# A Mamba-2 scan and a SwiGLU feed-forward in one kernel: banks of PSUM in pairs, 1024-wide operations, smaller weight pieces, and the first scan's preparation spread over the first gates

## Chip, cores, metric

One core of one Trainium2 chip. The metric is the device time of one execution in microseconds (us). All runs that are compared are of the state "fast"; the cores of the chip other than this one are idle.

## The reference

```python
# per batch and head, chunk by chunk (S = 768, N = 16, D = 32, 4 batches, 8 heads)
L = exp(cum_i - cum_j) * causal           # decay between two positions
M = (C @ B.T) * L                         # "products"
y = M @ x + (C @ state) * exp(cum)        # "outputs"
state = decay * state + sum_j (B_j x_j) * decay_from_j   # "states"

# bridge to 3072 tokens x 256, then
xn = x / sqrt(mean(x*x) + 1e-6) * rms_g
g = xn @ w_gate; val = xn @ w_val         # 256 -> 1536, float64 weights given as words
out = (silu(g) * val) @ w_out             # 1536 -> 256
```

## The kernel before

The tokens go through in six blocks of 512. A block has a gate loop of 12 steps (`gate_val`: two gate and two value matmuls, Silu on ACT, the hidden product `h` on DVE) and an output loop (`project`). The scan of the next block runs between the steps of the gate loop (`scan_steps`), for two pairs of tiles (a tile is 128 positions of one batch). Its exponentials of decays are prepared earlier: for the first blocks by mask-and-sum groups, matmuls that put the causal mask and the sums of logarithms into PSUM. DVE, ACT and POOL are the vector, scalar and GpSimd engines. The weights arrive as 64-bit numbers and are converted to 32 bits by DVE and ACT in pieces (`begin`, `finish`) during the head and block 0.

```python
def bank(name, shape=(128, 512)):                 # five single banks of PSUM
    return mm.tile(list(shape), FP32, tag="shared", bufs=5, name=name)
def pair_of_banks(name):                          # and one pair
    return mm.tile([P, 2, 512], FP32, tag="y", name=name)
# ... cut ...
pieces = [(n, c, w) for c, w in ((0, 128), (128, 128), (256, 256), (512, 512), (1024, 512))
          for n in "gv"]
pieces += [("o", c, 4) for c in range(0, NF, 4)]
# ... cut ...
def decays(g):                                    # exp of the decays of tile g
    L = pair_tile(g)
    for h in range(NH):
        nc.scalar.activation(out=L[:, h], in_=L[:, h], func=AF.Exp, bias=neg[:, c, k:k + 1])
    nc.gpsimd.affine_select(out=L, in_=L, ...)    # causal mask
def products(p, qs, gs=None):                     # qs: which 32-row groups of TensorE
    g = {q: bank("g%d" % q, (P, 2, 2 * P)) for q in qs}
    for i in range(2):
        for q in qs:
            nc.tensor.matmul(out=g[q][:, i], lhsT=s["T"][r, i, 0], rhs=...,
                             tile_position=(32 * q, 0), ...)
    for q in qs:
        nc.vector.tensor_tensor(out=L, in0=g[q], in1=L, op=ALU.mult)
# ... cut: in the loops, a pair's products are one call on all four row groups ...
[(products, p, range(4))],
[(states, p), (scale, q)],
[(turn, q, 0, cp)],
# ... cut: after block 0's output loop ...
for k in range(NT):
    put(blk, k, os[k])
for k in range(NT):
    decays(4 * (blk + 2) + k)
```

## Time and profile before

| | before |
|---|---|
| time | 495.72 us (median of 3), span 494.3 |
| TensorE busy | 465.0 us (94%) |
| first gate matmul | 41.9 us |
| block 0: gate loop, output loop | 64.4, 22.05 us |
| gate loops of blocks 1; 2, 3, 4; 5 | 61.9; 50.2, 50.1, 50.4; 41.2 us |

The gate loop of block 5 has no scan beside it and is 12 steps of 3.43 us with nothing between. Blocks 2 to 4 are the same plus a scan of some 9 us of TensorE. Blocks 0 and 1 show what stands beside that: block 0 is 14 us longer than block 2 and block 1 is 12. With the head of 42 us these are all that a change could win without taking work off TensorE. The lines are in the prediction.

### The profile page before, as it was taken

To read this page: it belongs to the slowest core of one execution; us is meant where nothing else is said; L and a number is where in the kernel's file an instruction comes from. 1 tells how busy PE (TensorE), PEld (TensorE's weight loads), DVE (VectorE), ACT (ScalarE), POOL (GpSimd) and SP (SyncE) were. 2 spreads that over 40 slices of the span, in tenths; PEclk is the share of its full clock that TensorE was granted. 3 is DMA by queue.
4 is the path that set the end of the run, shared out by engine and by line. 5 is a ranking of instruction groups with operands and counts; after the bars stand their busy time and mean duration, and the time that the engine had idled before them with its cause. 6 is when DMAs were issued, how large, how long until landed. Compare 5 with 4: busy or idle time off the path is not lost.

```text
span 494.3 us, 6025 instructions
## 1 busy us (share of the span) xinstructions
PE 465.0 (94%) x2410; PEld 274.8 (56%) x2410; DVE 156.2 (32%) x284; ACT 159.1 (32%) x325; POOL 42.1 (9%) x72
## 2 busy tenths in 40 slices
PE   6877869999939999999999999999999999999997
PEld 4543324468514447854447844448844448744486
DVE  3465998781014231114140124140124220121100
ACT  2327633530561213651314451223541220111100
POOL 3011000000030000220000310001110000000000
PEclk9989879999969999999999999999999999999999
DMA  9940455920470200063300071200000000000000
GB/s 138 184 113 2 170 170 181 176 78 1 72 141 1 86 0 12 23 83 98 86 1 11 23 112 69 86 2 11 30 3 0 1 1 21 21 1 0 0 12 32
DMA packets 85515, 27.85 MB, mean 56 GB/s; under 512 B 76048, under 2 KB 80336, under 8 KB 85488
## 3 DMA queue, kind: packets, MB, share of 16 engines
q1 hardware_dynamic: 81328, 27.21, 23.6%
q10 hardware_dynamic: 4160, 0.26, 0.6%
q8 instruction: 19, 0.31, 0.2%
q14 instruction: 8, 0.07, 0.0%
HBM read 24.22 MB, written 3.24 MB: 56 GB/s over the span
## 4 chain that ended last, share of the span: by engine, by line
PE 79%; issue 8%; DVE 3%; ACT 2%; POOL 2%; POOLq 0%; ACTq 0%; DVEq 0%
PE gate L478 25%; PE val L478 23%; PE o L489 21%; PE y L419 2%; PE g L357 2%; PE tp L343 2%; PE y L410 1%; POOL L L320 1%; DVE e L163 1%; PE ms L447 1%; PE rb L460 1%; PE A_ps L375 1%; DVE h L486 1%; DVE L L364 0%; POOL rs L452 0%
## 5 line engine op out<-in xcount | busy, mean ns | idle before, releaser
L478 PE MATMUL gate<-xn,wg 128*128 128x512 f32 x288 | 143.6, 622 | 6.2 <-DVE h L486 4.3
L478 PE MATMUL val<-xn,wv 128*128 128x512 f32 x288 | 137.6, 601 | 0.0
L489 PE MATMUL o<-wo,h 128*128 128x256 f32 x576 | 127.4, 380 | 0.0
L489 PEld LDWEIGHTS o<-wo,h 128*128 128x128 f32 x576 | 108.7, 190 | 16.9 <-issue 2.9
L486 DVE TENSOR_TENSOR h<-u,val 128x512 f32<-128x512 f32 x72 | 49.4, 686 | 208.7 <-PE val L478 141.8
L478 PEld LDWEIGHTS val<-xn,wv 128*128 128x128 f32 x288 | 56.1, 195 | 71.9 <-issue 68.5
L481 ACT ACTIVATE u<-gate 128x512 f32<-128x512 f32 x72 | 42.8, 596 | 134.0 <-PE gate L478 98.4
L478 PEld LDWEIGHTS gate<-xn,wg 128*128 128x128 f32 x288 | 52.0, 195 | 56.5 <-issue 44.1
L494 ACT COPY ob<-o 128x256 f32<-128x256 f32 x24 | 8.9, 372 | 107.3 <-PE o L489 89.5
L318 ACT ACTIVATE L<-L,neg 128x128 f32<-128x128 f32 x128 | 38.8, 389 | 0.0
L364 DVE TENSOR_TENSOR L<-g,L 128x512 f32<-128x512 f32 x48 | 30.0, 683 | 8.3 <-PE g L357 8.3
L436 POOL TENSOR_TENSOR sq<-sq 128x256 f32<-128x256 f32 x12 | 9.2, 770 | 254.6 <-ACT sq L435 254.6
L466 DVE SCALAR_TENSOR_TENSOR xn<-yt,gcol,rb 128x512 f32<-128x512 f32 (+1 forms) x14 | 8.8, 669 | 53.6 <-PE rb L460 50.2
L320 POOL TENSOR_SCALAR_AFFINE_SELECT L<-L 128x1024 f32<-128x1024 f32 x16 | 17.5, 1092 | 90.6 <-ACT L L318 90.6
L345 ACT COPY T<-tp 128x512 f32<-128x512 f32 x22 | 12.8, 583 | 33.0 <-PE tp L343 33.0
L435 ACT ACTIVATE sq<-y 128x512 f32<-128x512 f32 x12 | 7.2, 597 | 34.4 <-PE y L410 34.4
L357 PE MATMUL g<-T 32*128 32x256 f32 x192 | 17.8, 404 | 0.4 <-DVE h L486 0.2
L343 PE MATMUL tp<-ident,cp 128*128 128x128 f32 x48 | 9.5, 280 | 7.0 <-POOL cp L329 7.0
L357 PEld LDWEIGHTS g<-T 32*128 32x128 f32 x192 | 10.3, 184 | 10.3 <-issue 7.2
L151 ACT ACTIVATE e<-e,etop 128x1024 f32<-128x1024 int32 (+2 forms) x13 | 11.5, 885 | 10.0 <-DVE e L148 10.0
L419 PE MATMUL y<-L,xr 128*32 128x128 f32 x384 | 13.8, 288 | 0.0
L343 PEld LDWEIGHTS tp<-ident,cp 128*128 128x128 f32 x48 | 6.1, 143 | 13.1 <-POOL cp L329 7.6
(88 smaller groups left out, 234.9 us busy)
## 6 DMA issues: line engine op xcount, KB each, us to landing
L<-rowd SPq DMA_DIRECT2D x16, 512.0 KB, 5.2
xr<-in_x_dram SPq DMA_DIRECT2D x24, 128.0 KB, 3.3
wr<-in_moe_w_out_dram SPq DMA_DIRECT2D x3, 1024.0 KB, 5.4
out_dram<-ob SPq DMA_DIRECT2D x24, 128.0 KB, 1.7
wr<-in_moe_w_gate_dram SPq DMA_DIRECT2D x2, 1024.0 KB, 5.3
wr<-in_moe_w_val_dram SPq DMA_DIRECT2D x2, 1024.0 KB, 4.9
br<-in_B_dram SPq DMA_DIRECT2D x22, 64.0 KB, 3.0
cr<-in_C_dram SPq DMA_DIRECT2D x22, 64.0 KB, 2.9
```

What stands on the lines that cost most here:

```text
L151: nc.scalar.activation(out=ef, in_=e, func=AF.Relu, scale=-8.0, bias=etop)
L318: nc.scalar.activation(out=L[:, h], in_=L[:, h], func=AF.Exp, bias=neg[:, c, k:k + 1])
L320: nc.gpsimd.affine_select(out=L, in_=L, pattern=[[0, NH], [1, P]], compare_op=ALU.is_ge, fill=0.0, base=0, channel_multiplier=-1)
L343: nc.tensor.transpose(out=tp[:, k], in_=src.rearrange("p h n -> p (h n)"), identity=ident)
L345: copy(out=s["T"][:, i], in_=tp)
L357: nc.tensor.matmul(out=g[q][:, i], lhsT=s["T"][r, i, 0], rhs=s["T"][r, i, 1:3].rearrange("p t m -> p (t m)"), start=(i == 0), stop=True, t ...
L364: nc.vector.tensor_tensor(out=L, in0=g[q], in1=L, op=ALU.mult)
L419: nc.tensor.matmul(out=y[o:o + 32, h // 4, i * P:(i + 1) * P], lhsT=s["x"][:, i, h], rhs=Ls[p][:, i, h], start=opens, stop=True, tile_posi ...
L478: nc.tensor.matmul(out=dst, lhsT=w[:, t, fs], rhs=xns[blk][:, t], start=(t == 0), stop=(t == 1))
L481: nc.scalar.activation(out=u, in_=g, func=AF.Silu)
L486: nc.vector.tensor_tensor(out=h, in0=u, in1=v, op=ALU.mult)
L489: nc.tensor.matmul(out=o, lhsT=hs_[blk, f][:, k * P:(k + 1) * P], rhs=wo[:, f], start=(f == 0), stop=(f == NF - 1))
```

## The change

Its intent: keep TensorE fed in the head and in the first two blocks. PSUM is cut anew into two single banks and three pairs; gate and value share a pair, as do the two halves of other results, so that DVE and ACT work on 1024 elements at a time. The weights are converted in smaller pieces with deeper buffers. Block 1's mask-and-sum groups are spread between the first gates (before, they all stood ahead of them; its scan was beside block 0's gate loop already), and the exponentials of block 2 move into block 0's output loop. TensorE gets six dummy matmuls at the start. The core of the diff:

```diff
-        return mm.tile(list(shape), FP32, tag="shared", bufs=5, name=name)
+        return mm.tile(list(shape), FP32, tag="one", bufs=2, name=name)
-        return mm.tile([P, 2, 512], FP32, tag="y", name=name)
+        return mm.tile([P, 2, 512], FP32, tag="pair", bufs=3, name=name)
...
+    pieces = [(n, c, w) for c, w in [(0, 128), (128, 128)] + [(c, 256) for c in range(256, DF, 256)]
+    pieces += [("o", c, 2) for c in range(0, NF, 2)]
...
+    for k in range(6):
+        nc.tensor.matmul(out=idle[:, 0], lhsT=warm[:, 0:P], rhs=warm, start=True, stop=True)
...
-        for h in range(NH):
-            nc.scalar.activation(out=L[:, h], in_=L[:, h], func=AF.Exp, bias=neg[:, c, k:k + 1])
+        nc.vector.tensor_tensor(out=L, in0=L, in1=tok[...].to_broadcast([P, NH, P]), op=ALU.subtract)
+        nc.scalar.activation(out=L, in_=L, func=AF.Exp)
...
-            [(products, p, range(4))],
-            [(states, p), (scale, q)],
-            [(turn, q, 0, cp)],
-            [(outputs, p)],
-            [(turn, q, 1, cp)],
-            [(products, q, range(4))],
+            [(products, p, 0)],
+            [(products, p, 1), (pad, q, pl), (scale, q)],
+            [(states, p), (turn, q, 0, cp)],
+            [(outputs, p), (turn, q, 1, cp)],
+            [(products, q, 0)],
+            [(products, q, 1)],
...
+        if f in (5, 7, 9, 11):           # in block 0's output loop
+            decays(8 + (f - 5) // 2)
```

## The prediction

> **What bounds the kernel now.** I read, in this order: the page's busy rows, the busy time by stretch, the timeline around the two places where TensorE has holes, and the timeline of one undisturbed block. The span is 494.3 us; the timed median is 495.72, so 1.4 us lie outside the span.
>
> ```profile
> PE   6877869999939999999999999999999999999997
> PEclk9989879999969999999999999999999999999999
> ```
>
> Each digit is a fortieth of the span (12.4 us). TensorE is at 9 from the sixth slice on, but for one hole (the 3 in the twelfth slice, 136 to 148 us). So the kernel has two regimes: a head of some 75 us that is bound by latencies and conversions, and a rest that is bound by TensorE.
>
> ```profile
> 54.00:75.00 21.00, 16.50 (x44) 7.21 (x43) 19.92 (x26) 10.62 (x13) 0.00 (x0) 0.76 0.53 190
> 75.00:106.00 31.00, 31.00 (x194) 14.52 (x193) 26.01 (x36) 14.97 (x20) 2.00 (x2) 1.00 0.71 173
> 127.00:143.00 16.00, 8.95 (x27) 4.53 (x25) 0.00 (x0) 14.10 (x40) 5.12 (x8) 0.89 0.75 123
> 212.00:284.70 72.70, 72.70 (x376) 43.48 (x375) 17.59 (x33) 25.17 (x58) 7.75 (x11) 1.00 0.24 51
> ```
>
> (Columns: stretch, length, busy of PE, weight loads, DVE, ACT, POOL with counts, granted clock, DMA.) From 54 to 75 DVE is busy 19.9 of 21 us with converting the weights, and TensorE waits for it, partly at a lower clock (0.76). From 127 to 143 ACT is busy and TensorE is not. Block 2 (212 to 284.7) is TensorE without a hole.
>
> ```profile
> 69.36 3.78 PE L478 MATMUL gate<-xn,wg 128*128 128x512 f32 x4 [4.34 <-DVE h L486]
> ...
> 131.64 9.45 ACT L318 ACTIVATE L<-L,neg 128x128 f32<-128x128 f32 x32
> 141.11 1.28 ACT L481 ACT_TABLE_LOAD   x1
> 142.54 0.71 PE L343 MATMUL tp<-ident,cp 128*128 128x128 f32 x2 [7.05 <-POOL cp L329]
> 144.11 0.48 PE L343 MATMUL tp<-ident,Cd 128*128 128x128 f32 x1 [0.86 <-DVE Cd L332]
> 144.38 3.62 PE L478 MATMUL gate<-xn,wg 128*128 128x512 f32 x4
> ```
>
> The last four rows are the hole at the start of block 1: 32 small exponentials in ACT after block 0, a table load, then TensorE goes on at half speed (3.62 us for a gate that takes 1.9).
>
> From the chain and the timeline, TensorE's schedule is: first gate matmul 41.9; block 0's gates end 106.3; its output matmuls end 128.35; block 1 takes 84.1 (to 212.45); blocks 2, 3, 4 take 72.2, 72.1, 72.5; block 5, which has no scan beside it, 61.9 (to 491.2); copy and store 3.1. Sum 494.3.
>
> **What the Trainium skill says.** "TensorE: Matmul & The Clock Gate", Part 3, says that matmuls on different 32-row groups run at the same time, starting about 4 ns apart. The trace agrees: matmuls of `g` on four row groups start 7 ns apart, and the next four 216 ns later. This decides what splitting them costs. Its Part 1 says that the clock falls to half after an idle window of about 3.4 us; here the records show half speed for 3.4, 3.4, 6.8 and 10.2 us after the holes. "ScalarE: Activation LUTs", What ACT_TABLE_LOAD costs, gives about 1283 ns; every load here takes 1.28 us. "VectorE: DVE Perf Modes", The TRN2 errata, says that each operation pays a fixed cost, so wide ones are cheaper: a 512-wide exponential on ACT takes 608 ns here, the 128-wide one 295 at its pitch (9.45 / 32), so eight of those (2.36 us) become one of about 1.03 (estimate: 608 plus 512 elements at the slope (1149 - 722) / 512 = 0.83 ns of the ACT conversions).
>
> **Part 1: products of the scan, split in two.** Before, `products` of a pair takes all four row groups in one call; after, two calls with two row groups each, on either side of a gate. The trace before holds both forms, the small one in the head:
>
> ```profile
> 226.99 1.15 PE L357 MATMUL g<-T 32*128 32x256 f32 x16
> 228.07 1.98 PE L478 MATMUL gate<-xn,wg 128*128 128x512 f32 x4
> ...
> 22.30 1.13 PE L357 MATMUL g<-T 32*128 32x256 f32 x8
> 23.36 0.43 PE L375 MATMUL A_ps<-xr,Bd 128*32 128x64 f32 x16
> ```
>
> Sixteen instructions on four groups take 1.08 us to the next start, eight on two groups take 1.06. Half the groups means no saving: each call costs the same. The gate after it starts slower too: 1.91 in the chain in place of 1.72, 0.19. So one more call per pair is 1.08 + 0.19 = 1.27 us of TensorE, 2.54 per block, in each of the five blocks that have a scan beside them. DVE's 1024-wide multiplication (about 1.2 us for what took 2 x 0.62) is beside other work and gives nothing back. In blocks 1 to 4 TensorE is the bound, so this is a loss of 4 x 2.54 = 10.2 us; block 0's share is counted below.
>
> **Part 2: the hole of block 1.** The exponentials of block 2 move from after block 0's outputs into its output loop, at its steps 5, 7, 9 and 11, with subtraction on DVE (1.2 each) and one exponential each (1.03); the Silu table is loaded behind them. DVE and ACT idle in that loop now (DVE 4.6 of 21 us busy), so they fit. POOL's padding, for which TensorE waited 7.05 us, then comes some 10 us before it is wanted. The block should fall to the 72.2 of block 2: gain 84.1 - 72.2 = 11.9, less the 2.54 of part 1.
>
> **Part 3: conversions in block 0.** DVE's work per element is the same: 4.87 us for a 1024-wide piece (0.60 + 0.72 + 1.15 + 1.26 + 1.14, starts in the timeline), 2.73 for a 512-wide one. Of the output weights four of six pieces move into the output loop (4 x 2.73 = 10.9 us). DVE's gate loop from the third step on holds 8 gate/value pieces (21.8), parts of two output pieces (4.1), ten hidden products (6), scan (about 7): 39 us, while TensorE has 10 x 3.43 + 9 + 2.5 = about 46. So DVE should no longer bind, save at single pieces.
>
> **Part 4: the head.** TensorE is warmed with 6 dummy matmuls (about 2.6 us at half speed, while it waits 3.2 for `a` anyway). The mask-and-sum groups `e` for four tiles take 2.93 us (34.17 to 37.10). For two tiles I get 2 x 0.216 masks, 8 steps of 0.112, 2 wide passes of 0.43 and about 0.3 of changes: 2.5, again half the groups for nearly the same time. There are four such calls before (11.7 us); after, one of four tiles and six of two (17.9). But only the first and three small ones stand before the outputs of pair 1. Walking the head in TensorE's order with these durations I get: first sums done 9.3 (11.3 before), outputs of pair 1 done 27.3 (34.2 before). Then the norm, now once: square and POOL to 28.8, sums to 29.4, POOL power (1.02) to 30.7, one small `e` group to 31.9, transposes, DVE's two multiplications to 34.0. First gate 34.0 (41.9 before).
>
> Then comes what eats that gain. Before gate 2 can start it needs the pair of banks of gate 0, which waits for `h`, Silu, the Silu table, and ahead of these in ACT the last of block 1's four exponentials. TensorE: gate 0 to 37.4, two `e` groups to 42.4, gate 1 to 45.8, last `e` group to 48.3. Then exponential 1.03, table 1.28, Silu 0.6, `h` 0.68 and handovers: gate 2 at 52.1, against 53.9 before. TensorE idles over 3 us, so I add one cold window (3.4 us at half speed, 1.7 lost). From there 46 us of TensorE work end block 0's gates at 99.6 (106.3 before): gain 6.7. The output loop is 22.05 as before, plus about 0.5 where DVE just misses an output piece at steps 8 and 10.
>
> **Sum.** 99.6 + 22.55 + (72.2 + 2.54) + (216.8 + 7.6) + 61.9 + 3.1 = 486.3 span; with 1.4 outside it 487.7. I say 487.5: 1.7% faster. The gain of 18.6 in the first two blocks (6.7 + 11.9) is more than half paid away by splitting the products in blocks 1 to 4.
>
> **Rivals.**
> - *Splitting costs nothing* (the calls overlap with the gate, or TensorE takes both with its queue): the profile speaks against it (1.06 against 1.08, and a full gate needs all row groups). It would give about 477.
> - *Silu and table do not hold gate 2, no cold window*: for it, the warm start and fewer holes; against it, ACT's strict order. It would save up to 5 us: 482 to 484.
> - *Three pairs are too few*: a gate waits for the third allocation before it (`h`, the multiplication, the copy of `y`). In the full loop each is read about 1 to 2 us after its matmuls and wanted 3 or more later, so I expect no waits; a wait of 0.3 per gate would add 15 us: 502.
> - *The output loop of block 0 starves*: the spread transfers now come after the loads of block 2 on one queue, and DVE, in order, would hold the output weights behind a subtraction that waits for them. They take 5.2 us to land, 8.7 us are there. If late: 2 to 5 us, 490 to 493.
>
> **Range and chances.** The later blocks are counted from rows and good to a microsecond or two; the head is walked by hand and good to some 3. The range is 482.5 to 491.5. The line of 2% is at 485.8, half a deviation below my figure: faster 0.33, same 0.65, slower 0.02.
>
> **What would show it.** Right: `g` as calls of eight instructions with 1.06 to 1.1 us to the next start, blocks 2 to 4 at 74.7 without holes; block 1 also 74.7, with no wait for POOL; a first gate near 34, a hole of some 3 us before gate 2, with a clock below 1 after it; gates of block 0 ending near 99.6. Wrong: blocks 2 to 4 still at 72.2 (part 1 falls, and about 10 us more are won), waits of gates for `h` in every block (three pairs are too few), or block 0's gates ending after 103 (DVE still binds).

## The result

489.61 us (median of 4, 489.46 to 490.0) against 495.94 of the kernel before on the same chip; ratio 0.987 (0.9854 to 0.9888). All ratios here are the mean time of one kernel's fast runs over that of the other's fast runs of the same rounds, so not quite the ratio of the medians. The time lies in the range that was stated, 2 us above the figure, and on the predicted side of the line of 2%.

The slices of the changed kernel's page, for the two rows of the prediction's first fence:

```profile
PE   8989989999999999999999999999999999999997
PEclk9978999999999999999999999999999999999999
```

The hole in the twelfth slice is gone. The clock dips to 7 in the third slice, where the kernel before had 8. By stretch (length, then busy time of PE, weight loads, DVE, ACT, POOL, granted clock, DMA share, GB/s):

```profile
57.00:75.00 18.00, 16.56 (x64) 8.03 (x63) 17.69 (x32) 10.48 (x18) 0.00 (x0) 1.00 0.34 118
75.00:101.00 26.00, 26.00 (x171) 12.29 (x170) 19.74 (x36) 12.15 (x22) 1.45 (x2) 1.00 0.60 126
101.00:124.40 23.40, 22.46 (x109) 19.25 (x108) 20.48 (x30) 11.32 (x14) 4.00 (x4) 1.00 0.28 91
124.40:199.30 74.90, 74.90 (x374) 44.29 (x373) 22.10 (x32) 19.79 (x33) 8.56 (x12) 1.00 0.25 55
199.30:274.00 74.70, 74.70 (x374) 44.24 (x373) 22.36 (x33) 19.32 (x30) 8.01 (x11) 1.00 0.23 50
```

The fourth line is block 1 and the fifth block 2, both without a hole. The output loop of block 0 (third line) now holds 20.5 us of DVE work, where it held 4.6. Blocks 1 and 2 take 74.9 and 74.6 us; block 2 took 72.2. Why they are longer is in the timeline of block 2, to be held against the first two lines of the prediction's last fence:

```profile
213.88 1.13 PE L378 MATMUL g<-T 32*128 32x256 f32 x8
214.94 1.98 PE L498 MATMUL gate<-xn,wg 128*128 128x512 f32 x4
216.76 1.88 PE L498 MATMUL gate<-xn,wv 128*128 128x512 f32 x4
218.57 1.13 PE L378 MATMUL g<-T 32*128 32x256 f32 x8
```

Eight instructions, 1.06 us to the next start, and twice per pair of tiles.

By stretches of TensorE, from the first matmul of one to the first of the next (us):

| stretch | before | after | difference | predicted |
|---|---|---|---|---|
| to the first gate | 41.9 | 35.5 | -6.4 | -7.9 |
| block 0, gates | 64.4 | 65.3 | +0.9 | +1.2 |
| block 0, outputs | 22.05 | 23.5 | +1.5 | +0.5 |
| block 1 | 83.9 | 74.9 | -9.0 | -9.4 |
| blocks 2 to 4 | 216.8 | 224.0 | +7.2 | +7.6 |
| block 5 and tail | 65.2 | 65.1 | -0.1 | 0 |

The sum is -5.9, and -6.0 by the spans (494.3 to 488.3). The predicted column sums to -8.0.

The timeline of the changed kernel's head, where TensorE's waits are:

```profile
28.95 0.61 PE L468 MATMUL ms<-mean,sq 128*128 128x1 f32 x4 [1.05 <-POOL sq L457]
29.94 1.92 PE L301 MATMUL e<-rows,sel 32*128 32x128 f32 x16
35.45 3.78 PE L498 MATMUL gate<-xn,wg 128*128 128x512 f32 x4 [0.84 <-DVE xn L487]
...
53.56 1.28 ACT L598 ACT_TABLE_LOAD   x1
53.60 1.98 PE L498 MATMUL gate<-xn,wg 128*128 128x512 f32 x4 [0.54 <-ACT L L313]
54.85 1.09 ACT L506 ACTIVATE u<-gate 128x512 f32<-128x512 f32 x2
55.48 0.69 DVE L511 TENSOR_TENSOR h<-u,gate 128x512 f32<-128x512 f32 x1 [5.14 <-ACT u L506]
```

The clock records give half speed from 30.1 to 40.4 us: the `e` group at 29.94 takes 1.92 us where another takes 1.16, and the first gate 3.78 where 1.98 is usual. The last four lines show that gate 2 (53.60) starts before the Silu of gate 0 (54.85) and before its `h` (55.48). The prediction had it wait for them.

### The profile page after: what moved, and what is told of

Read it like the earlier page. It is cut to its first block, busy times and chain, and to the rows that moved or that the text cites. A ratio compares the mean times of both kernels' runs of the same rounds, so it can differ in the third digit from the quotient of the medians.

```text
span 488.3 us, 5897 instructions
## 1 busy us (share of the span) xinstructions
PE 478.6 (98%) x2420; PEld 281.5 (58%) x2420; DVE 178.5 (37%) x308; ACT 140.4 (29%) x224; POOL 41.9 (9%) x70
## 4 chain that ended last, share of the span: by engine, by line
PE 92%; DVE 5%; ACT 1%; issue 0%; POOL 0%; ACTq 0%
PE gate L498 50%; PE o L514 23%; PE g L378 5%; PE y L440 2%; PE tp L358 2%; PE e L301 2%; PE y L431 2%; PE e L306 1%; DVE m L155 1%; PE e L287 1%; PE ms L468 1%; DVE e L161 1%; PE A_ps L396 1%; PE rb L481 1%; PE idle L245 1%; DVE h L511 1%
## 5 line engine op out<-in xcount | busy, mean ns | idle before, releaser
L498 PE MATMUL gate<-xn,wv 128*128 128x512 f32 x288 | 136.0, 595 | 0.0
L511 DVE TENSOR_TENSOR h<-u,gate 128x512 f32<-128x512 f32 x72 | 49.4, 687 | 208.4 <-ACT u L506 208.4
L498 PEld LDWEIGHTS gate<-xn,wv 128*128 128x128 f32 x288 | 55.1, 191 | 69.8 <-issue 69.8
L498 PEld LDWEIGHTS gate<-xn,wg 128*128 128x128 f32 x288 | 51.0, 191 | 53.6 <-issue 48.3
L384 DVE TENSOR_TENSOR L<-g,L 128x1024 f32<-128x1024 f32 x24 | 29.3, 1219 | 5.2 <-PE g L378 4.5
L326 DVE TENSOR_TENSOR L<-L,tok 128x1024 f32<-128x1024 f32 x16 | 22.1, 1400 | 0.0
L329 ACT ACTIVATE L<-L 128x1024 f32<-128x1024 f32 x16 | 16.9, 1059 | 3.9 <-DVE L L326 3.8
L149 ACT ACTIVATE e<-e,etop 128x512 f32<-128x512 int32 (+1 forms) x20 | 13.5, 674 | 11.7 <-DVE e L146 11.7
L161 DVE SCALAR_TENSOR_TENSOR e<-wr,e 128x512 int32<-128x512 int32 (+1 forms) x20 | 12.7, 633 | 7.4 <-ACT e L150 7.4
L155 DVE SCALAR_TENSOR_TENSOR m<-wr,m 128x512 f32<-128x512 uint32 (+1 forms) x20 | 13.6, 678 | 0.7
L150 ACT ACTIVATE e<-e,einf 128x512 int32<-128x512 f32 (+1 forms) x20 | 13.6, 679 | 0.7
```

Source lines behind the costliest of these rows:

```text
L150: nc.scalar.activation(out=e, in_=ef, func=AF.Relu, scale=-1.0, bias=einf)
L155: nc.vector.scalar_tensor_tensor(out=f, in0=lo.bitcast(U32), scalar=2.0 ** -32, in1=m, op0=ALU.mult, op1=ALU.add)
L161: nc.vector.scalar_tensor_tensor(out=e, in0=hi, scalar=-2 ** 31, in1=e, op0=ALU.bitwise_and, op1=ALU.bitwise_or)
L326: nc.vector.tensor_tensor(out=L, in0=L, in1=tok[:, c, b * NH:(b + 1) * NH].unsqueeze(2).to_broadcast([P, NH, P]), op=ALU.subtract)
L329: nc.scalar.activation(out=L, in_=L, func=AF.Exp)
L384: nc.vector.tensor_tensor(out=L, in0=g.rearrange("p q (i m) -> p q i m", i=2), in1=L, op=ALU.mult)
```

## The experiments

Ten kernels, all correct. Where a run's time is given with two values, its executions fell into two groups by the clock. "Window" is a stretch at half clock in the records. They ran in other rounds than the changed kernel; the kernel before had medians of 496.2 to 496.8 us in them, so differences under about 1 us between kernels of different rounds are read from the traces.

**Products again in one call (e1_merged).** Into two pairs of banks at once.

```diff
-            [(products, p, 0)],
-            [(products, p, 1), (pad, q, pl), (scale, q)],
+            [(products_both, p)],        # for i: for q in range(4): matmul ...
+            [(pad, q, pl), (scale, q)],
...                                       # the same for pair q
```

> The changed kernel with one part undone: in the loops the products of a pair are again one call on all four row groups (now into two pairs of banks at once, then two 1024-wide multiplications). Theory (half the row groups cost the same time): each of the ten pairs saves 1.27 us, blocks 1 to 4 fall from 74.6-74.9 to 72.1-72.4 us, the time to about 477, ratio to the kernel before 0.962. Rival A (three pairs are too few, and the split was needed so that gates find a free pair): the next gate waits for the hidden product after every merged call, 1 us or more each, and the time stays at 487 or above. Rival B (the 2.5 us more per block come from something else, such as the 1024-wide operations or the new order): nothing changes, 489.

490.36 us, ratio 0.9881: no gain. Both the theory and rival A hold, each in its place. The gate loops of blocks 1 to 4 fell from 52.7 to 51.0 us on average, 1.7 each and 6.8 in all. The timeline of its block 1:

```profile
146.05 1.15 PE L394 MATMUL g<-T 32*128 32x256 f32 x16
147.53 1.98 PE L515 MATMUL gate<-xn,wg 128*128 128x512 f32 x4 [0.34 <-DVE h L528]
```

The call of 16 costs what one of 8 did, but the next gate now waits 0.34 us, as the call holds two of the three pairs and the third is the one from which `h` is still being computed. In block 0, where DVE also converts weights, that wait is ten times as long, and windows come with it (from 66.95 and from 90.84 us):

```profile
67.29 3.48 PE L515 MATMUL gate<-xn,wg 128*128 128x512 f32 x4 [3.68 <-DVE h L528]
...
90.17 3.10 PE L515 MATMUL gate<-xn,wg 128*128 128x512 f32 x4 [3.12 <-DVE h L528]
```

Block 0's gates took 72.5 us (65.3 in the changed kernel). The split is thus what three pairs need in block 0, and a loss everywhere else.

That `h` is so late has a second cause, in the groups of instructions (busy, mean ns, idle time before, what ended it), the kernel before and the changed one:

```profile
L486 DVE TENSOR_TENSOR h<-u,val 128x512 f32<-128x512 f32 x72 | 49.4, 686 | 208.7 <-PE val L478 141.8
```

```profile
L511 DVE TENSOR_TENSOR h<-u,gate 128x512 f32<-128x512 f32 x72 | 49.4, 687 | 208.4 <-ACT u L506 208.4
```

Before, `h` waited mostly for the value matmuls; Silu had run beside them. Now gate and value are one tile, Silu starts only when the value matmuls have ended, and `h` always waits for Silu, so it comes some 0.6 us later. Nothing pays for that while pairs are free; the merged call pays.

**The split alone, in the kernel before (e2_split_before).** Steps as in the changed kernel, with `(products, p, (0, 1))` and `(products, p, (2, 3))` in single banks.

> The kernel before with that part alone: products in two calls of two row groups, in the step order of the changed kernel. Theory: ten more calls at 1.27 us, 508 to 509 us; blocks 2 to 4 from 72.2 to 74.7. Rival B: 496, unchanged.

503.46 us, ratio 1.014. The gate loops of blocks 2 to 4 went from 50.2, 50.1, 50.4 to 52.6, 52.5, 52.8: 2.4 us each, exactly as in the changed kernel, so rival B falls. The total is 5 us less than I expected, as block 0's gates (62.6 for 64.4) and block 1 (63.6 for 61.9) have holes that absorb the additional calls.

**Exponentials of block 2 back behind the output loop (e3_late_decays).**

```diff
-        if f in (5, 7, 9, 11):
-            decays(8 + (f - 5) // 2)
     for k in range(NT):
         put(0, k, os[k])
+    for k in range(NT):
+        decays(8 + k)
```

> The changed kernel with block 2's exponentials moved back behind block 0's output loop, still 1024 wide. Theory (the hole of block 1 came from where they stood): a wait of TensorE for the padding on POOL comes back at the first transposition of block 1, about 4 us plus a clock window, block 1 at 79 to 83 us in place of 74.9, and the 0.9 us wait for an output weight piece in block 0's output loop goes; time 493 to 497. Rival C (the narrow form was the cause, and wide operations alone would have removed the hole): block 1 stays below 76 us, time 488 to 490.

495.26 us (three of four runs 494.7 to 496.0; one without a window in the head, 490.2), ratio 0.9956. The hole of block 1 is back, although the operations are wide:

```profile
133.35 0.71 PE L358 MATMUL tp<-ident,cp 128*128 128x128 f32 x2 [3.06 <-POOL cp L337]
134.62 0.47 PE L358 MATMUL tp<-ident,Cd 128*128 128x128 f32 x1 [0.56 <-DVE Cd L346]
134.88 3.62 PE L498 MATMUL gate<-xn,wg 128*128 128x512 f32 x4
```

Block 1's gates took 59.8 us (52.8), and block 0's output loop 22.05 (23.5). So the move wins 7.0 us and costs 1.5. Rival C falls: wide operations alone do not remove the hole. But they make it smaller. With the narrow ones at the same old place, in a scan that is split too, block 1's gates took 63.6 us (e2_split_before), and TensorE waited there 7.9 us, here 3.6. So the width is worth about 3.8 us at the old place; the two kernels differ in other parts of the change too, so this is less strictly shown than the 7.0.

**Narrow exponentials at the new places (e8_narrow).**

```diff
-        nc.vector.tensor_tensor(out=L, in0=L, in1=tok[...], op=ALU.subtract)
-        nc.scalar.activation(out=L, in_=L, func=AF.Exp)
+        for h in range(NH):
+            nc.scalar.activation(out=L[:, h], in_=L[:, h], func=AF.Exp, bias=tok[:, c, k:k + 1])
...                                       # and tok is stored with the other sign
```

> The changed kernel with the exponentials of blocks 2 to 5 in the narrow form of before (eight 128-wide ones with a bias, no subtraction on DVE) at their new places. Theory: the width is off the path: ACT gets 1.3 us more per group and has the room, DVE is freed of 1.2 to 1.4 us per group, so TensorE's wait for an output weight piece in block 0's output loop goes; blocks 1 to 4 unchanged, time 488 to 489.6. Rival H (the wide form is what let the exponentials fit into the output loop): ACT runs behind, block 1 waits, 492 or more.

Two runs with the window at 490.6 and 490.7, two without at 485.5. Against the changed kernel with the window (489.6) that is up to 1 us more (0.6 by the spans of the traces), not the half microsecond less that I expected: block 0's output loop stayed at 23.45, with a wait of 1.1 us for an output weight piece. That piece now queued in ACT, where its first conversion step stood behind eight narrow exponentials:

```profile
115.24 2.45 ACT L328 ACTIVATE L<-L,tok 128x128 f32<-128x128 f32 x8
117.59 0.71 ACT L149 ACTIVATE e<-e,etop 128x512 f32<-128x512 int32 x1
```

Block 1's gates took 53.6 us (52.8). The main point stands: the place of the wide exponentials wins 7 us, while their width, at the new place, wins under 1.

**Without the dummy matmuls (e4_no_warm).**

```diff
-    for k in range(6):
-        nc.tensor.matmul(out=idle[:, 0], lhsT=warm[:, 0:P], rhs=warm, start=True, stop=True)
```

> The changed kernel without the six dummy matmuls. Theory: TensorE then starts cold as in the kernel before, the clock reaches full speed some 3 us later (about 9.9 us in place of 6.2), and about 4 us of work that ran fast runs at half speed: 1 to 2 us longer, 490.5 to 491.5. Rival D (the head hides it, as it waits for data and conversions): within 0.3 us of 489.6.

486.35 us, faster than the changed kernel by 3.3: both the theory and rival D missed. The cold start is there and costs 0.7 us (the first sums end at 9.79 us in place of 9.06). But the window from 30 to 40 us is missing in the profiled run (its first gate takes 1.98 us) and, by time and mean clock, in two more (486.2 to 486.4), and shorter in two (mean clock 0.992 and 0.993, 488.5 and 488.6; their timelines were not kept). So the window is not the same in every execution, and by this run costs some 4 us; between runs of one kernel with and without it, 5.1 (e8_narrow) and 5.3 (e5_hybrid). Over all runs here with dummy matmuls and an unchanged norm it came, by the mean clock, in 20 of 24.

**Gaps of the norm filled (e6_fill).** Two of block 1's mask-and-sum groups move up.

```diff
+    ex = masked()
+    sums([(2, 0, ex)])
+    decay(2, 0, ex)
     norm_sums(0, range(NT))
+    ey = masked()
+    sums([(3, 0, ey)])
+    decay(3, 0, ey)
...
     norm_apply(0, range(NT))
```

> The changed kernel with two of block 1's mask-and-sum groups moved up into the gaps of the norm of block 0 (one ahead of the sums of squares, one ahead of the transposes), nothing else. Theory: the half-speed window from 30 to 40 us in every run of the changed kernel (it makes the group after it 1.9 us longer and the first gate 2.7) is set off by TensorE's 1.0 us wait for the squares and its light work about it; filled, the clock stays full, the first gate starts at 33 to 34, block 0's gates end near 96, time 484.5 to 486. Rival F: the window comes anyway, as its cause is not these gaps; mean clock stays 0.989, time 488.5 to 490.

484.36 us, ratio 0.9752, and mean clock 1.0 in all four runs that were timed.

```profile
27.40 1.16 PE L301 MATMUL e<-rows,sel 32*128 32x128 f32 x16
28.40 1.03 PE L306 MATMUL e<-sel,rows 32*128 32x512 f32 x4
29.35 1.05 PE L468 MATMUL ms<-mean,sq 128*128 128x1 f32 x8
30.27 0.59 PE L287 MATMUL e<-never,ident 128*128 128x512 bf16 x2
...
34.33 1.95 PE L498 MATMUL gate<-xn,wg 128*128 128x512 f32 x4 [0.93 <-DVE xn L487]
```

The wait for the squares is gone, TensorE is busy up to 33 us, and the first gate runs at full speed. Block 0's gates end at 94.7 us (100.8). Rival F falls: in the same rounds on the same chip two kernels with the old norm (e5_hybrid, e8_narrow) had the window in 5 of 8 runs.

**Both (e6b_fill_no_warm).**

> The same without the six dummy matmuls. The run without them showed three of five runs with no half-speed window and 486.2 us, two with a short one and 488.5. Theory (the gaps decide, the dummy matmuls only speed up the first 3 us): no windows in any run, 0.7 us behind the filled kernel with dummy matmuls. Rival G (the dummy matmuls themselves bring the later window about): no window here, but the filled kernel with dummy matmuls still has one, so this one is faster by 3 us.

485.21 us (one of four runs at a mean clock of 0.996), 0.85 behind e6_fill. The gaps decide, as in the theory, and rival G falls as it was stated, since e6_fill has no window either. What the dummy matmuls are worth is not shown here: the medians differ by less than this kernel's own runs do (484.05 to 486.02), and in the two traces the first gates start 0.08 us apart. Why the window came less often without them in e4_no_warm stays open; the clock's windows do not stand at the same time in every execution.

**Merged products in blocks 1 to 4 only (e5_hybrid).**

```diff
+            [(products, p, 0)] if blk == 1 else [(products_both, p)],
+            ([(products, p, 1)] if blk == 1 else []) + [(pad, q, pl), (scale, q)],
```

> The changed kernel with the products merged into one call on four row groups in the loops of blocks 1 to 4 only; block 0's loop keeps the two calls. The first run of the merged form gained 1.7 us in each of blocks 1 to 4 (not 2.5, as a wait of 0.33 us for the hidden product follows every merged call) and lost 7.2 us in block 0. Theory: both effects are separate, so block 0's gates take 65.3 us as in the changed kernel, the loops of blocks 1 to 4 take 50.9 in place of 52.6, time 482 to 483.5. Rival: block 0's loss was an accident of clock windows and not of the merged call; then this run gains the same 6.8 us and does not tell, but a run of it whose clock record has windows in block 0's loop would.

483.24 us (three runs with the window; the one without, 478.0). Block 0's gates took 65.4, the loops of blocks 1 to 4 50.8 to 51.2, as expected. The rival that e1_merged lost in block 0 by clock windows alone is not decided by this run, but by e1_merged's trace: TensorE waited 8.95 us in block 0's gates there and 2.82 in the changed kernel, while its two windows there, 3.4 us each at half speed, can have cost 3.4 together.

**Large weight pieces (e10_large_pieces).** Pieces of before, with the buffers of before: three large ones and two for the conversion.

```diff
-    pieces = [... [(0, 128), (128, 128)] + [(c, 256) for c in range(256, DF, 256)] ...]
+    pieces = [... [(0, 128), (128, 128), (256, 256), (512, 512), (1024, 512)] ...]
-    pieces += [("o", c, 2) for c in range(0, NF, 2)]
+    pieces += [("o", c, 4) for c in range(0, NF, 4)]
-    plan = ["ff", "bbf", "f", "bbf", "f", "bbf", "f", "bbf", "f", "b", "bf", ""]
+    plan = ["ff", "bbf", "f", "", "bb", "f", "f", "", "b", "", "bf", ""]
```

> The changed kernel with the weight pieces of before (up to 512 columns, 4 output rows at a time) and the buffers that then fit (three large ones and two for the conversion, in place of six and three). Theory (piece size matters only where a gate waits for a piece): DVE has 0.6 us less per 1024 elements, but finishes in portions of 2.4 us ahead of hidden products, so block 0's gates take 65 to 69 us in place of 65.3, block 0's output loop 22 to 24, blocks 1 to 4 unchanged: 489 to 493. Rival: the small pieces are what took the wait of 4.3 us out of block 0; then a wait of that size comes back at a gate in the middle of block 0, 493 to 496.

492.96 us, ratio 0.9935. Block 0's gates took 69.6 us, the output loop 22.05. The additional 4.3 us in the gate loop are waits of 0.9 to 1.4 us behind DVE's and ACT's larger portions (3.3 in sum; such waits sum to 1.4 in the changed kernel) and a window of 6.8 us (3.4 lost) at 63 us, which the changed kernel does not have. The rival's wait of over 4 us did not come back. So the small pieces with their deeper buffers win about 4 us in the gates and give 1.5 back in the output loop; pieces, buffers and plan were changed together, and my plan for the large ones is one of many, so the figure is for this plan.

**What helped, together (e9_best).** Merged products in blocks 1 to 4, the filled gaps, and the subtractions at steps 7, 9, 10 and 11 of the output loop.

> What helped, together: products merged in the loops of blocks 1 to 4, two mask-and-sum groups in the gaps of the norm, and in block 0's output loop the exponentials' subtractions on DVE at steps 7, 9, 10 and 11 in place of 5, 7, 9 and 11, so that the output weight pieces come first. Theory: the gains add, 5.3 (no half-speed window) + 6.8 (1.7 in each of four blocks) + 1.0 to 1.5 (output loop 22.1 to 22.6 in place of 23.5) off 489.6: 476 to 477, ratio to the kernel before 0.960. Rival: with the later subtractions block 1 waits for POOL again and gives the last gain back: 477.5 to 479.

477.03 us (476.91 to 478.07), ratio to the kernel before 0.962 (0.9606 to 0.9637), clock 1.0 in all five runs. The output loop fell to 22.2, block 0's gates end at 94.3, and blocks 2 to 4 are as in e5_hybrid. Block 1 is not: its gates took 52.6 us (51.2 there), with a wait that e5_hybrid does not have:

```profile
125.07 0.33 PE L358 MATMUL tp<-ident,Cd 128*128 128x128 f32 x1 [1.26 <-DVE Cd L346]
```

The last exponential now runs 1.6 us into block 1, Silu's table is loaded behind it, 5.6 us after block 1's first gate (3.6 in the changed kernel), and DVE reaches `Cd` only after the `h` that waits for this Silu. So the rival was right about the cost, though the wait came by ACT and DVE and not by POOL: moving the subtractions won 1.3 us in the output loop and lost 1.5 in block 1. The kernel beats the one before and the changed one by its other two parts.

## Why the prediction was right

- *Part 1, the price of split products.* 2.54 us per block was predicted, 2.4 measured, in the changed kernel and alone in the kernel before. The 0.14 came off because states and outputs now share their steps with a transposition: gates and values grew by 0.19 us per block, where I had added 0.38, while the transpositions grew by 0.11. This is why the change moved the time so little: 7.2 us of what the first blocks won went into blocks 2 to 4, and 2.4 more into block 1. The rival that splitting is free fell.
- *Part 2, the hole of block 1.* -9.4 predicted, -9.0 measured; no wait for POOL remained, and e3_late_decays brought it back. The step is shown. Its parts, by block 1's gates: the split cost 1.7 (e2_split_before), the width won about 3.8 and the place 7.0 (e3_late_decays).
- *Part 3, conversions.* Block 0's gates took 65.3 us, 65.6 predicted, and DVE no longer held TensorE for long; the longest wait for it there was 1.1 us. That the two lengths meet is in part luck, by the terms of part 4: without the window the same stretch took 62.9 (e4_no_warm). From gate 2 on the work itself was as counted, 45.7 us for 45.8, and waits of 1.4 came on top. In the output loop I was 1 us short: 23.5 for 22.55. The pieces came later than I had counted, with 1.46 us for one 512-wide operation that usually takes 0.69, beside POOL's mask. No subtraction waited for its transfer, so the rival of the starved output loop is not what happened. With the subtractions later the wait is gone, but block 1 pays for it (e9_best).
- *Part 4, the head.* The walk up to the end of pair 1's outputs was right (27.4, predicted 27.3). After that two terms were wrong and cancelled. First, gate 2 was to wait for `h` of gate 0, as I took the three pairs to be handed out in turn. The trace shows it waiting for the last exponential, so it had the pair of the last `e` group. The hole was 0.54 us and not over 3. On this point the second rival (Silu and table do not hold gate 2) was right. Second, I put a window of 3.4 us (1.7 lost) after gate 2. It came at 30.1 us, in the norm, was 10.2 us long and cost about 5 (5.1 between runs of e8_narrow; e6_fill: 5.2 less, with the same work in another order). The first gate therefore started at 35.5 and not at 34.0, and was slow itself; e6_fill and e9_best, without the window, have it at 34.3 and 33.9.
- *The rival of too few pairs* was rightly put aside for this kernel: in blocks 1 to 4 no gate waited. But it comes true as soon as the split is undone (e1_merged), and so gives the split a use, which I had not seen.

The 2 us between 487.5 and 489.6 are the window, at most 3.3 us beyond the 1.7 that I had allowed, and the output loop (1.0), less the hole before gate 2 that did not come.

## What to carry to other kernels

Here a call on two of the four row groups took the time of one on all four (1.06 and 1.08 us to the next start), so splitting a call for the sake of buffers is paid in full wherever TensorE is the bound; split only in the stage where the buffers are short. Before moving work off a stage, look at whether its wait is set by the place of the work or by its width; here the place won 7 us with wide operations, while the width won about 3.8 at the old place and under 1 at the new one. A light stretch between dense ones, here the norm, was a good place for matmuls that are needed soon anyway: the same work in another order won 5 us, most of it by keeping the clock up.

## What the Trainium skill lacked or had wrong

- "TensorE: Matmul & The Clock Gate", Part 1, puts the half-rate state after at least one idle window of about 3.4 us. In the changed kernel TensorE waited at most 1.05 us at a time in the 10 us before the clock fell at 30.1 us; it stayed low for 10.2 us, and filling the gaps kept the mean clock at 1.0 in 12 of 13 timed runs (e6_fill, e9_best, e6b_fill_no_warm; 0.996 in the other). In the kernel before, windows began at 30.4 and 54.3 us, with no wait over 1.93 us in the 10 us before them. Light activity with short gaps was enough. The same Part, under "A second HAM failure mode: psum-queue depth-cycling", does say that frequent micro-idles made the clock fall in another kernel; it gives no length for them. The same kernel without a change of code ran with and without the window (e8_narrow: 490.6 and 485.5 us).
- The same page calls the event records unreliable, which agrees: the record of e4_no_warm has no event and a mean clock of 1.000, while its first four masks start 0.42 us apart and later ones 0.22. So a mean clock of 1.000 alone does not show that there was no window; where this text says so, the time or the durations of the gates agree. The page on traces does not say that a mean clock can leave out the cold start.
- No page gives the price of the two sides of row tiling against each other, though "TensorEngine Tiling (Array Packing)", Gotcha 1, names the pressure on PSUM. "PSUM — Partial Sum Buffer", PSUM bank collisions raise a hardware error, says that different row tiles may not use one bank at the same time; what follows is that four row groups at once hold four banks until DVE has read them. With three pairs this made the next gate wait 0.34 us in a quiet loop and up to 3.68 us in a busy one (e1_merged), against 1.2 us for the second call (2.4 per block, two calls).
